# Requests for a weight tile one step sooner, and four casts moved ahead of two copies, in a fused linear-attention and low-rank-mixer kernel

## The chip, the cores and the metric

One core of a Trainium2 chip runs the whole kernel. The core has five engines that run side by side, each with its instructions in a fixed order: TensorE (PE in the profile; its weight loads are PEld), VectorE (DVE), ScalarE (ACT), GpSimd (POOL) and SyncE (SP). SP, and in places ACT, ask for transfers; sixteen DMA engines carry them out. The metric is the time of one execution on the device, in microseconds (us).

## The reference, cut to what matters

Two blocks follow each other. The first is linear attention with decay, 4 batches, 8 heads, 768 positions, head size 64, worked in blocks of 64 positions with a running state:

```python
intra = (qb @ kb.T * Dmask) @ vb                 # per head; Dmask = lam ** (i - j), i >= j
inter = (qb * lam_pow) @ kv_state
out[:, :, block] = intra + inter
kv_state = lam ** 64 * kv_state + (kb * rev_pow).T @ vb
```

Its output, heads side by side, is x with 4 x 768 rows of 512. The second block mixes positions by a low-rank product (rank 32) and then channels by a two-layer network (512 to 2048 to 512):

```python
u = x + (x.T @ U @ V).T
out = u + np.maximum(u @ w_ch1, 0) @ w_ch2
```

U, V and both weight matrices arrive in double precision, so the kernel has to turn their 64-bit words into single precision itself.

## The kernel before, in words

The kernel keeps near-single precision on TensorE by splitting each operand of the large products into a high part and a low part (and a difference of them), so each large product is three matmuls.

It has two halves. The front (up to about 120 us) walks through 24 steps, one for each 128 rows: step s belongs to batch s // 6 and is its row tile c = s % 6 (NT is 6, NS is 24). The back is two long runs of matmuls, u @ w_ch1 (lines 833 and 844) and relu(...) @ w_ch2 (lines 965 to 969).

The order of the front is written out by hand, as a list of pieces per step (lines 648 to 681), under a manual schedule: an engine's instructions stand in the order in which the pieces issue them. What a step does, in that order:

- **turn, split** (lines 592 on): transposes of a finished row tile of u and their split into high and low parts, for the first product.
- **prep(s + 1)** (line 371): TensorE transposes q and k of the next step (L361); ScalarE copies them from PSUM, q first, then k (L367, qt and kt); SP asks for a later q.
- **next_of_low**: the next of a list of pieces for the low-rank rows of the batch just finished. For batches 0 to 2 the list has two pieces (lines 525 to 543). The first, own, casts four groups of rows to their high parts on ScalarE (L528), with the low parts subtracted on POOL behind each (L529). The second, other, copies the rows to a second set of partitions by four small transfers on SP (L539).
- **scale** on POOL (L392 for q, L381 for k), **mixed** on VectorE (L574).
- **intra, state, inter**: the block's products on TensorE. intra (L455) multiplies the masked scores with v, state (L427) makes the running state, inter (L466) uses the state before. A copy on ScalarE (L472) takes the result from PSUM. next_v asks for a later v on ScalarE's queue.
- the second **next_of_low**, in the first step of a batch.
- **scores(s + 1)** on TensorE (L408), and **masked(s + 1)** on VectorE (L417): the scores of the next step times the decay mask. So L408, L417 and the next step's L455 follow each other across three engines.
- **low** (L482, the low-rank product of a finished batch), **mix** (L562, the mixing of positions for a row tile of the batch before; for its first tile it stands at the end of the second step).
- **aside(s)**: a slice of side work, given by a table (lines 738 to 747). It holds the conversion of U, V and of the first two tiles of w_ch1.
- **store** of u and **next_k** on SP.

The side work of a tile of w_ch1 has twelve pieces: four requests for its words, a quarter each (L146, 128 KB, on SP); an extraction of the exponents on VectorE (one, L166), with two operations on ScalarE behind (L173, L174); the mantissa (L155); and two, three, four, five, six, seven, which assemble and split the value. The table says for each piece the step whose aside holds it. NS there means the pieces left over for after the front. In steps after the sixth the aside stands between scores and masked, so a piece of it on VectorE runs ahead of the mask of the next step.

The words of consecutive tiles alternate between two buffers. Tile 0's words are requested in steps 8 to 11 and extracted in step 12; tile 1's table row is the one that changes.

Of the kernel before, what the change touches and what calls it, by code (L numbers as in the profile page):

```python
# [18 lines left out]
def kernel(  # L19
# [32 lines left out]
    NT = S // P  # L52
# [7 lines left out]
    NS = B * NT  # L60
# [142 lines left out]
    def split_steps(tile_of, src, in_parts=False, scale=None, apart=False):  # L203

        st = {}

        def dst():
            if "w" not in st:
                st["w"] = wconv.tile([P, C], FP32, tag="wf", name="wf")
            return st["w"]  # L210

        def five():
            st["o"] = o = tile_of()
            st["t"] = o[:, 0, :].bitcast(FP32)
            on_scalar(lambda: nc.scalar.mul(o[:, 0, :], st["w"], NEAR))  # L215

        def six():
            w, low = st["w"], st["o"][:, 1, :]
            st["low"] = low.bitcast(FP32) if scale is None else w
            nc.vector.tensor_tensor(  # L220
                out=low if scale is None else w, in0=w, in1=st["t"], op=ALU.subtract
            )
            if scale is not None:
                on_scalar(lambda: nc.scalar.mul(low, w, scale))

        def seven():
            nc.vector.scalar_tensor_tensor(
                st["o"][:, 2, :], st["t"], -E, st["low"], ALU.mult, ALU.add
            )

        return weight_steps(dst, src, C, in_parts=in_parts, apart=apart) + [five, six, seven]
# [3 lines left out]
    def w1_steps(ft, in_parts=False, apart=False):  # L235
        def tile_of():
            w1v[ft] = w1_pool.tile([P, 3, C], F32R, tag="w1", name="w1")
            return w1v[ft]

        cols = moe_w_ch1[:, ft * P : (ft + 1) * P].rearrange("(c p) f -> p c f", p=P)  # L240
        return split_steps(tile_of, cols, in_parts, apart=apart)
# [407 lines left out]
    for s in range(NS):  # L649
        b, c = divmod(s, NT)  # L650
        done = s - NT - 1
        more = s + 1 < NS
        turns = done > 0 and (done - 1) // TG < FG
        mixes = 0 <= done < NS - NT - 1
        rows = c == 0 and b > 0
        step = [("fade", s)] * (c > 0)
        step += [("mix", done)] * (mixes and c != 1) + [("turn", done - 1)] * turns
        step += [("split", done - 1)] * turns
        step += [("prep", s + 1)] * more
        step += [("mix", done + 1)] * (not more)  # L660
        step += [("next_of_low", b - 1)] * rows
        step += [("scale", s + 1)] * more
        step += [("mixed", done)] * (mixes and c != 1)
        step += [("late", s - 1)] * (1 < s < NT - 1 or s > NT)
        step += [("turned", done - 2)] * (done > 1 and c == 1)
        step += [("mixed", done + 1)] * (not more)
        both = [("intra", s), ("state", s)]
        step += (both if s > NT else both[::-1]) + [("next_v", s), ("inter", s)]
        step += [("next_of_low", b - 1)] * rows
        step += [("late", s)] * (s < 2 or s in (NT - 1, NT))  # L670
        step += [("turned", done - 1)] * (done > 0 and c > 0)
        step += [("mix", done), ("mixed", done)] * (mixes and c == 1)
        step += [("scores", s + 1)] * more
        step += [("low", b)] * (more and c == NT - 1)
        step += [("aside", s)] * (0 < s < NT - 2 or s > NT)
        step += [("masked", s + 1)] * more
        step += [("low_rows", b)] * (more and c == NT - 1)
        step += [("aside", s)] * (s in (0, NT - 2, NT - 1, NT))
        step += [("store", done)] * (done >= 0 and done // TG < FG)
        step += [("next_k", s)] * (s > 0)  # L680
        pieces += step
# [15 lines left out]
    def v_steps():  # L697

        st = {}

        def dst():
            if "v" not in st:
                st["v"] = wconv.tile([P, C], FP32, tag="wf", name="vf")[0 : 2 * R, 0:SH]
            return st["v"]

        def parts(gs):
            for half in range(2):
                rows, cols = slice(half * R, (half + 1) * R), slice(half * SH, (half + 1) * SH)
                for g in gs:
                    yield v_hl[g * R : (g + 1) * R, cols], rows  # L710

        def five():
            st["t"] = t = wconv.tile([P, C], FP32, tag="wt", name="vt")[0 : 2 * R, 0:SH]
            nc.vector.tensor_scalar(
                t.bitcast(U32), st["v"].bitcast(U32), HI, None, ALU.bitwise_and
            )
            on_scalar(high)

        def high():
            for out, rows in parts((0, 2)):  # L720
                nc.scalar.copy(out, st["t"][rows])

        def low(g, engine):
            for out, rows in parts((g,)):
                engine.tensor_tensor(
                    out=out, in0=st["v"][rows], in1=st["t"][rows], op=ALU.subtract
                )

        halves = [moe_V[:, half * SH : (half + 1) * SH] for half in range(2)]
        return weight_steps(dst, halves, SH, 2 * R, in_parts=True) + [  # L730
            five, lambda: low(1, nc.vector), lambda: low(3, nc.gpsimd),
        ]
# [6 lines left out]
    for steps, at in (  # L739
        (u_side, (-1, 1, 1, 2, 2)),  # L740
        (v_steps(), (0, 0, 3, 3, 4, 4, 4, 5, 5)),
        (w1_steps(0, True, True), (8, 9, 10, 11, 12, 14, 15, 16, 17, 17, 20, 21)),
        (w1_steps(1, True, True), (15, 16, 17, 18, 18, 22, 23, NS, NS, NS, NS, NS)),
    ):
        assert len(steps) == len(at)
        for step, n in zip(steps, at):
            side.setdefault(n, []).append(step)
# [140 lines left out]
    c0, b = NS - NT, B - 1  # L888
# [180 lines left out]
```

## Time and profile before

| | |
|---|---|
| median of the runs | 659.63 us (659.31 to 661.56) |
| profiled execution | 657.43 us |
| its span in the trace | 655.6 us |
| TensorE busy | 640.6 us (98%) |
| TensorE's weight loads busy | 539.5 us (82%) |
| VectorE, ScalarE, POOL busy | 435.8, 268.6, 116.4 us |
| moved by DMA | 131.69 MB, mean 201 GB/s |
| requests for words of w_ch1 in quarters | 8 of 128 KB, 5.1 us to landing (median) |
| row copies L539 | 12 of 32 KB, 2.1 us to landing (median) |

Times in the text are counted from the start of the span. A line of the timeline gives start, duration, engine, source line, operation, output and inputs, and how many instructions are merged; in square brackets stands how long the engine was idle before it and what ended that. "SPq" and "ACTq" are requests for transfers, "PEld" the weight loads that go ahead of matmuls. In a line of the totals of waits stand the waiting engine and line, what it waited for, the total, the number of waits and the longest. "issue" means that no event shown in the profile ended the wait.

### The profile page before, as it was taken

The page shows a single profiled execution, that of the slowest core. Times are in us where ns is not written, and L with a number is a line of the kernel's source. Part 1 is how long each engine was busy: PE and PEld are TensorE (multiplying, and loading weights), DVE is VectorE, ACT ScalarE, POOL GpSimd, SP SyncE. Part 2 cuts the span into 40 slices and gives each one's busy share as a digit, 9 for nine tenths or more (in the row PEclk, how much of TensorE's full clock was granted, in tenths as well). Part 3 has the DMA queues.
Part 4 walks back from the last instruction along what each step waited for, and adds up shares of the span by engine and source line. Part 5 has one row for each costly group of instructions (what it writes and reads, how often), then busy time and mean ns, then how long its engine had stood idle before and what let it go on. Part 6 is the DMA issues. An engine that isn't in the chain of part 4 may idle for free.

```text
span 655.6 us, 13402 instructions
## 1 busy us (share of the span) xinstructions
PE 640.6 (98%) x5242; PEld 539.5 (82%) x5242; DVE 435.8 (66%) x713; ACT 268.6 (41%) x497; POOL 116.4 (18%) x104
## 2 busy tenths in 40 slices
PE   8999979999999999999999999999999999999997
PEld 7889968778888888888888888888888888888886
DVE  6766857676997777777798244585575665855854
ACT  4666756434664444444455131332232322322320
POOL 4475966331000000000000000030030210300300
PEclk9999998999999999999999999999999999999999
DMA  9989995155787556555576999865363363453521
GB/s 227 241 197 259 236 239 130 50 201 170 262 287 253 211 210 211 209 212 210 211 253 255 332 323 379 292 216 173 98 215 108 116 211 97 147 176 94 180 81 64
DMA packets 132737, 131.69 MB, mean 201 GB/s; under 512 B 81538, under 2 KB 90754, under 8 KB 132674
## 3 DMA queue, kind: packets, MB, share of 16 engines
q1 hardware_dynamic: 107552, 124.41, 58.4%
q10 hardware_dynamic: 25122, 6.42, 4.4%
q8 instruction: 41, 0.67, 0.4%
q14 instruction: 22, 0.18, 0.1%
HBM read 80.09 MB, written 50.33 MB: 199 GB/s over the span
## 4 chain that ended last, share of the span: by engine, by line
PE 93%; DVE 2%; DMA 1%; ACT 1%; issue 1%; POOL 0%; SPq 0%; ACTq 0%; DVEq 0%
PE pz L833 26%; PE pz L965 13%; PE pz L967 13%; PE pd L969 13%; PE pd L844 13%; PE px L455 3%; PE pss L408 3%; PE px L466 2%; PE pqk L361 1%; PE pkv L427 1%; PE pm L562 1%; DMA qraw<-in_q_dram 1%; PE pp L482 1%; PE pm L625 1%; DMA vp<-vp 0%
## 5 line engine op out<-in xcount | busy, mean ns | idle before, releaser
L833 PE MATMUL pz<-u_hl,w 128*128 128x512 f32 x768 | 184.5, 390 | 0.0
L833 PEld LDWEIGHTS pz<-u_hl,w 128*128 128x128 f32 x768 | 143.7, 188 | 30.0 <-ACT r L840 0.3
L967 PE MATMUL pz<-w_hl,m 128*128 128x512 f32 x384 | 148.6, 389 | 0.0
L965 PE MATMUL pz<-w_hl,m 128*128 128x512 f32 x384 | 148.2, 389 | 0.0
L969 PE MATMUL pd<-w_d,m 128*128 128x512 f32 x384 | 147.4, 389 | 0.0
L948 ACT ACTIVATE m<-rm 128x512 fp32r<-128x512 f32 x96 | 60.6, 632 | 183.1 <-PE pd L969 122.9
L949 DVE SCALAR_TENSOR_TENSOR m<-rm,m 128x512 fp32r<-128x512 f32 x96 | 71.5, 747 | 96.0 <-ACT m L948 96.0
L994 POOL TENSOR_TENSOR o<-o,u 128x512 f32<-128x512 f32 x20 | 29.7, 1521 | 433.3 <-DVE o L990 433.3
L849 DVE SCALAR_TENSOR_TENSOR r<-pd,r 128x512 f32<-128x512 f32 x96 | 61.7, 685 | 60.4 <-ACT r L840 48.2
L844 PE MATMUL pd<-u_d,w 128*128 128x512 f32 x384 | 95.9, 390 | 0.0
L969 PEld LDWEIGHTS pd<-w_d,m 128*128 128x128 f32 x384 | 72.1, 188 | 15.4 <-DVE m L950 0.3
L967 PEld LDWEIGHTS pz<-w_hl,m 128*128 128x128 f32 x384 | 72.1, 188 | 15.1
L965 PEld LDWEIGHTS pz<-w_hl,m 128*128 128x128 f32 x384 | 72.1, 188 | 14.7
L844 PEld LDWEIGHTS pd<-u_d,w 128*128 128x128 f32 x384 | 71.9, 188 | 14.8
L840 ACT ACTIVATE r<-pz 128x512 f32<-128x512 f32 x96 | 51.7, 590 | 64.4 <-PE pz L833 64.4
L950 DVE SCALAR_TENSOR_TENSOR m<-m 128x512 fp32r<-128x512 f32 x96 | 74.7, 780 | 3.0
L417 DVE TENSOR_TENSOR sm<-pss,mask 128x512 f32<-128x512 f32 x48 | 30.9, 684 | 16.7 <-PE pss L408 16.7
L215 ACT ACTIVATE w<-wf 128x512 fp32r<-128x512 f32 x32 | 20.3, 634 | 38.6 <-DVE wf L197 30.7
L455 PE MATMUL px<-vraw,sm 128*64 128x64 f32 x768 | 28.7, 229 | 5.6 <-issue 5.5
L455 PEld LDWEIGHTS px<-vraw,sm 128*64 128x64 f32 x768 | 25.8, 141 | 7.3 <-issue 5.8
L173 ACT ACTIVATE sc<-sc,ends 128x512 f32<-128x512 uint32 x30 | 21.6, 720 | 22.8 <-DVE sc L166 22.8
L408 PE MATMUL pss<-qt,kt 64*128 64x128 f32 x384 | 28.8, 289 | 0.0
(89 smaller groups left out, 608.5 us busy)
## 6 DMA issues: line engine op xcount, KB each, us to landing
r_d<-r SPq DMA_DIRECT2D x96, 256.0 KB, 2.4
rm<-r_d SPq DMA_DIRECT2D x96, 256.0 KB, 2.7
words<-in_moe_w_ch_dram SPq DMA_DIRECT2D x30, 512.0 KB, 4.3
w_d<-w SPq DMA_DIRECT2D x16, 768.0 KB, 3.4
w_hl<-w_d SPq DMA_DIRECT2D x16, 512.0 KB, 5.8
u_d<-x_nat SPq DMA_DIRECT2D x24, 256.0 KB, 4.0
u<-u_d SPq DMA_DIRECT2D x24, 256.0 KB, 4.3
qraw<-in_q_dram SPq DMA_DIRECT2D x23, 256.0 KB, 4.8
```

What stands on the lines that cost most here:

```text
L408: nc.tensor.matmul(out=pss[:, x, a, :], lhsT=kt[half[x], a, :], rhs=qt[half[x], a, :], start=True, stop=True,)
L455: nc.tensor.matmul(out=px[half[t], x, a, :], lhsT=sm[:, x, a, half[t]], rhs=vr[:, 2 * a + x, :], start=(a == 0), stop=(alone and a == HP - 1),
L833: nc.tensor.matmul(out=like(acc[g][0], g), lhsT=w[:, n, ct, :], rhs=columns(uhl[g][:, n], g, ct), start=(ct == 0 and n == 0), stop=(ct == ...
L840: nc.scalar.mul(rs[g], acc[g][0], 4096.0 + 1.0)
L844: nc.tensor.matmul(out=like(acc[g][1], g), lhsT=w[:, 2, ct, :], rhs=columns(ud[g], g, ct), start=(ct == 0), stop=(ct == CT - 1),)
L849: nc.vector.scalar_tensor_tensor(rs[g], acc[g][1], 4096.0, rs[g], ALU.mult, ALU.add)
L948: nc.scalar.activation(out=m[:, 0], in_=r, func=AF.Relu, scale=NEAR)
L949: nc.vector.scalar_tensor_tensor(m[:, 1], r, 0.0, hi, ALU.max, ALU.subtract)
L950: nc.vector.scalar_tensor_tensor(m[:, 2], hi, E, low, ALU.mult, ALU.subtract)
L965: nc.tensor.matmul(out=pz, lhsT=m[:, 0, cols], rhs=hl[:, 0], start=first, stop=False)
L967: nc.tensor.matmul(out=pz, lhsT=m[:, 1, cols], rhs=hl[:, 1], start=False, stop=end)
L969: nc.tensor.matmul(out=pd, lhsT=m[:, 2, cols], rhs=dd, start=first, stop=end)
```

## The change

Two edits. In the table, the four requests for tile 1's words move from steps 15, 16, 17, 18 to 14, 15, 16, 17; the extraction stays in step 18. In the list of pieces, for step 6 (the first step of the second batch, s == NT) the first next_of_low stands ahead of prep instead of behind it, so that ScalarE's four casts L528 come before its copies L367 of q and k for step 7; steps 12 and 18 keep the order they had.

```diff
         step += [("split", done - 1)] * turns
+        step += [("next_of_low", b - 1)] * (s == NT)
         step += [("prep", s + 1)] * more
         step += [("mix", done + 1)] * (not more)
-        step += [("next_of_low", b - 1)] * rows
+        step += [("next_of_low", b - 1)] * (rows and s > NT)
         step += [("scale", s + 1)] * more
...
         (w1_steps(0, True, True), (8, 9, 10, 11, 12, 14, 15, 16, 17, 17, 20, 21)),
-        (w1_steps(1, True, True), (15, 16, 17, 18, 18, 22, 23, NS, NS, NS, NS, NS)),
+        (w1_steps(1, True, True), (14, 15, 16, 17, 18, 22, 23, NS, NS, NS, NS, NS)),
```

TensorE, VectorE and POOL have the same instructions in the same order in both kernels. On ScalarE only the six instructions named change places. On SP the first request moves ahead of the store of u in step 14, each of the others likewise one step up, and none is left behind the four row copies of step 18.

## The prediction

> **What bounds the kernel now.** I read the page first, then the totals of waits, the chain, the timeline round the two places that the change touches, and a table of stretches. Three times are in play: the profiled execution took 657.43 us, its trace spans 655.6 us, and the median of the runs is 659.63 us (659.31 to 661.56), 2.2 above the profiled one. I work in the trace's own times and carry the difference to the median.
>
> The page's busy times, and the shares of the chain that ended last:
>
> ```profile
> PE 640.6 (98%) x5242; PEld 539.5 (82%) x5242; DVE 435.8 (66%) x713; ACT 268.6 (41%) x497; POOL 116.4 (18%) x104
> PE 93%; DVE 2%; DMA 1%; ACT 1%; issue 1%; POOL 0%; SPq 0%; ACTq 0%; DVEq 0%
> ```
>
> TensorE is the bound from end to end, so an edit on other engines matters only where TensorE stands still or runs slowly. From 152 us to the end the chain is matmuls of the two products; there is nothing there for this change. The totals of waits say where TensorE stands still:
>
> ```profile
> PE px L455 <- issue: 5.5, 3, 4.8
> DVE sc L166 <- DMA words<-in_moe_w_ch_dram: 5.0, 1, 5.0
> ...
> PE pm L562 <- DMA vp<-vp: 1.2, 1, 1.2
> ```
>
> One wait of 4.8 us before the intra-block products (L455), one of 5.0 us of VectorE for words of a weight tile, and one of 1.2 us for the low-rank rows. The timeline (start, duration, what) shows that the first two are one event, in step 18 (first block of the last batch):
>
> ```profile
> 86.03 2.17 SPq L146 DMA_DIRECT2D words<-in_moe_w_ch_dram  x1
> ...
> 92.56 1.16 PE L408 MATMUL pss<-qt,kt 64*128 64x128 f32 x16
> 92.56 3.03 SPq L539 DMA_DIRECT2D vp<-vp  x4
> ...
> 95.64 0.58 SPq L146 DMA_DIRECT2D words<-in_moe_w_ch_dram  x1
> ...
> 98.10 0.43 DVE L166 TENSOR_SCALAR sc<-words 128x512 uint32<-128x512 uint32 x1 [5.01 <-DMA words<-in_moe_w_ch_dram]
> 98.44 1.28 DVE L417 TENSOR_TENSOR sm<-pss,mask 128x512 f32<-128x512 f32 x2
> ```
>
> The reader sees a queue inside a queue. The fourth request for words stands on SP behind four row copies (L539, 3.03 us), so it goes out at 95.64 and lands at 97.98. VectorE, in order, waits for it from 93.08 to 98.10, and the masking of step 19 (L417), whose scores are ready at 93.72, stands behind. L455 needs that mask.
>
> **Part one: the four requests a step sooner.** Nothing is added: four requests of 128 KB go out in steps 14 to 17 in place of 15 to 18, each ahead of its step's store of u and the next k and q. On VectorE, ScalarE and POOL this part moves nothing. In step 18 only the extraction (L166) is left, behind the request of step 17, which stood third before: asked at 86.03, landed at 92.12, 6.09 us later. L166 could start at 93.08 anyway, and takes 0.43; the mask waits for the scores until 93.72. The words may thus land as late as 93.72 - 0.43 = 93.29 at no cost: 1.17 us of room.
>
> What the step costs then need not be guessed, since step 12, the same step one batch earlier, does the same work with its words in hand (the only one of the two with a wait is 18). Its lines, and the stretches of step 18 and 19 (length, busy times, then the granted clock of TensorE, DMA share, GB/s):
>
> ```profile
> 65.59 0.42 DVE L166 TENSOR_SCALAR sc<-words 128x512 uint32<-128x512 uint32 x1
> ...
> 67.14 1.24 PE L455 MATMUL px<-vraw,sm 128*64 128x64 f32 x32
> ...
> 72.23 1.15 PE L455 MATMUL px<-vraw,sm 128*64 128x64 f32 x32
> ```
>
> ```profile
> 94.46:99.23 4.77, 0.01 (x2) 0.03 (x1) 1.13 (x3) 1.79 (x4) 3.24 (x3) 0.74 0.63 174
> 99.23:102.06 2.83, 2.83 (x52) 2.71 (x55) 1.09 (x2) 0.77 (x2) 0.00 (x0) 0.50 0.55 123
> 102.06:105.82 3.76, 3.76 (x82) 3.49 (x84) 2.65 (x7) 2.01 (x6) 3.54 (x3) 0.80 0.46 113
> ```
>
> With the words there, the mask starts at 93.74 and L455 of step 19 follows 0.79 later, as in step 12 (mask 66.35, L455 67.14): 94.53 in place of 99.23, 4.70 us sooner. From there to L455 of the next step took 72.23 - 67.14 = 5.09 in the batch before, but 105.75 - 99.23 = 6.52 now, because the clock was granted at 0.50 and 0.80 after the standstill: 1.43 more. So part one is worth 4.70 + 1.43 = 6.13 us; I take 6.1.
>
> Bounds. Below: SP pushes the loads of steps 14 to 17 back by at most the longest issue of such a request seen in steps 15 to 17, 2.25 us; the words then land at 94.4 and cost 1.1 of the gain: 5.0. If their flight is also as long as the longest of the front (a k load, 7.30 against 6.09), another 1.2 goes: 3.8. Above: 6.2, since TensorE already works back to back in step 13. I take 6.1 because the steps 8 to 11, each with one request as 14 to 17 will be, ran at 4.31 us a step without a wait for a transfer.
>
> At one place the size hangs on a rule. The rows show the slow clock after an idle stretch of 4.77 us, and none after the 1.2 us wait. The Trainium skill, "TensorE: Matmul & The Clock Gate", section "Part 1: The HAM clock gate", says that the clock falls to half after an idle window of about 3.4 us, that the window runs free of the kernel, and that the slow time therefore varies from run to run. By that rule an unprofiled run might pay less than 1.43, and the sum of both parts could be as low as 5.4; by the trace's rows it is 6.8, and I keep the rows.
>
> The rest of the saved time must survive to the end. Loads for steps 19 to 23 hang on buffers that the same steps free, so they come earlier too; the copies of the low-rank rows for step 19 land at 96.86, and TensorE would reach their use (L562) at 94.53 + 69.50 - 67.14 = 96.89. That is met with nothing to spare, and a wait here, were a copy to take the longest landing of its kind (3.3 us from 95.01), would cost 1.4.
>
> **Part two: the rows' high parts first, in step 6.** Four casts (L528), 0.30 us each and 0.32 apart, now come ahead of the copies of q and k (L367). Nothing else is reordered on ScalarE, and no queue is passed on SP or POOL; their waits end sooner. These lines show the place:
>
> ```profile
> 35.51 0.59 ACT L367 COPY kt<-pqk 128x512 f32<-128x512 f32 x1
> ...
> 36.12 0.62 ACT L528 CAST vp<-p_f 32x128 fp32r<-32x128 f32 x2
> ...
> 36.41 1.16 PE L408 MATMUL pss<-qt,kt 64*128 64x128 f32 x16
> ...
> 42.23 0.50 PE L562 MATMUL pm<-vp 64*128 64x256 f32 x3 [1.17 <-DMA vp<-vp]
> ```
>
> The casts can start at 34.70 (the rows leave PSUM at 34.66) in place of 36.12. Loss: q's copy moves to 35.98 and k's ends at 37.06, 0.96 late; the scores of step 7 (L408), now at 36.41, start at 37.10, 0.69 late, and TensorE's next steps with them. Gain: the four POOL subtractions behind the casts and the four copies on SP behind those start about 1.4 sooner, so the last copy lands at about 42.18 - 1.4 = 40.8. TensorE reaches the second matmul of the mix at 40.86 (the first starts at 40.67, and one takes about 0.19) + 0.69 = 41.55, finds its rows there, and goes on where it went on at 42.23: 0.68 us sooner. The POOL product of q (L392) moves forward with its queue and stays clear of its use. Bounds: +1.17 if the scores lose nothing after all; -0.69 if the last copy, whose record is missing, keeps its old landing (the chain's 42.18) and TensorE's later work finds no slack. I take 0.7, next to the worked row.
>
> **Sum.** 6.1 + 0.7 = 6.8 us. The profiled execution would take 657.43 - 6.8 = 650.6, and the median, 2.2 above it, 659.63 - 6.8 = 652.8 us.
>
> **The rivals.**
> *The gain comes in part.* The words land late or the row copies become the next wait. For it: 1.17 us of room, no room at L562, and a stretch from 72.23 to 90.60 with the DMA engines full (285 GB/s, against 265 in steps 8 to 11). Against: steps 12 and 13. With 3.8 from part one and nothing from part two, 659.63 - 3.8 = 655.8.
>
> *The change does nothing.* L455 waits for something else, such as v or the earlier output copy. v landed at 87.49 and the copy ended at 94.11, while the first half of the mask ended at 99.08, just before 99.23. That nearly excludes it; the time would stay at 659.6.
>
> *Slower, by the DMA queues.* The engines are full in steps 14 to 17, and a fifth transfer a step could hold back q, k and v. It decides when k of step 18, asked at 76.10 behind the new request, lands after TensorE wants it: landing 80.55, use 84.80, so 4.25 us of room. The extra 128 KB at 285 GB/s is 0.46 us. Only if each of the four steps lost 2.5 us would it reach 659.63 + 10 - 6.8 = 662.8. The Trainium skill, "DMA: Bandwidth & Descriptors", section "Issuing engines are not separate DMA queues", speaks on this side: transfers of all queues share the same 16 engines and interleave, so asking sooner makes no bandwidth. The trace agrees that the engines are full there, and shows that the loads have the room.
>
> **How the numbers follow.** 0.5% of this kernel, 3.3 us, is about what a measurement can tell from no change. Chances: forecast 0.79, gain in part 0.10, nothing 0.05, slower 0.06. The forecast's own range is 651 to 654.5: 6.8 give or take the bounds nearest to it, with the runs' spread of about 1. The range given reaches from 650.5 (part two at its upper bound, 1.17, and a median closer to the profiled time) to 656.5, which takes in the partial gain. Faster by over 0.5% (below 656.3): 0.79 and nearly all of the partial case, 0.88; same 0.06; slower 0.06.
>
> **What would show it.** In the new profile L166 of step 18 starts within half a microsecond of 92.4 (93.08 less part two), with no wait for words; the longest wait before L455 is under 1 us; the granted clock stays at 1.00 between 92 and 105; L455 of steps 19 and 20 are about 5.1 apart. For part two, scores of step 7 at about 37.1 and L562 with no wait for the rows. It would be wrong if words land after about 92.6 in the new times, if L562 of step 19 waits, or if TensorE waits for q, k or v between 72 and 92.

## The result, and the profile after

The changed kernel took 650.97 us in the median (650.55 to 651.89, four runs), the kernel before 660.6 beside it (659.31 to 662.2). The ratio is 0.9855, with a 95% interval of 0.9827 to 0.9883: 9.6 us less, between 7.7 and 11.4. The ratios, here and below, leave out runs in a slower state of the chip, of which there was one, the 661.33 us of fourth_first. The measured median lies 1.8 us below the predicted 652.8, inside the wide range (650.5 to 656.5) and at the lower edge of the forecast's own (651 to 654.5). The profiled execution took 651.21 us, with a span of 649.4; the one before had 655.6, so between the two traces there are 6.2 us. The rest of this text is about what lies between 6.2 and 9.6, and about which of the two edits gave what.

Busy times and the shares of the chain, from the page of the kernel after:

```profile
PE 638.7 (98%) x5242; PEld 537.8 (83%) x5242; DVE 435.7 (67%) x713; ACT 268.4 (41%) x497; POOL 116.3 (18%) x104
PE 93%; DMA 3%; DVE 1%; ACT 1%; issue 1%; ACTq 0%; DVEq 0%; SPq 0%
```

TensorE still bounds the kernel, with the same number of instructions; VectorE's share of the chain went from 2% to 1%, and that of transfers from 1% to 3%, most of it where the second product starts (386 to 402 us). Of the totals of waits, two lines answer to those shown of before:

```profile
PE px L455 <- issue: 1.9, 4, 0.7
...
PE pss L408 <- ACT kt L367: 0.6, 1, 0.6
```

The waits of L166 for words (5.0 us) and of L562 for the row copies (1.2) are gone, and the longest wait before L455 fell from 4.8 to 0.7. A new one of 0.6 stands before the scores: step 7 now waits for k's copy. The timeline of the kernel after round step 18:

```profile
85.60 2.13 SPq L146 DMA_DIRECT2D words<-in_moe_w_ch_dram  x1
...
90.02 1.15 PE L455 MATMUL px<-vraw,sm 128*64 128x64 f32 x32
...
91.97 1.16 PE L408 MATMUL pss<-qt,kt 64*128 64x128 f32 x16
91.98 2.95 SPq L539 DMA_DIRECT2D vp<-vp  x4
92.42 0.42 DVE L166 TENSOR_SCALAR sc<-words 128x512 uint32<-128x512 uint32 x1
...
93.18 1.29 DVE L417 TENSOR_TENSOR sm<-pss,mask 128x512 f32<-128x512 f32 x2 [0.34 <-PE pss L408]
93.97 1.24 PE L455 MATMUL px<-vraw,sm 128*64 128x64 f32 x32
...
98.81 1.15 PE L455 MATMUL px<-vraw,sm 128*64 128x64 f32 x32
```

The last request goes out at 85.60, its words land at 90.86, and L166 takes them at 92.42 without a wait. The mask now waits for the scores and not for VectorE, and L455 of step 19 follows the mask 0.79 later. L455 of step 18 to that of step 20 took 15.15 us before and 8.80 now. In the timeline of the kernel before, step 18 begins here; step 20 follows at 105.75:

```profile
90.60 1.18 PE L455 MATMUL px<-vraw,sm 128*64 128x64 f32 x32
```

In the stretches of the kernel after between the starts of L455 in steps 18, 19, 20 and 21 (length, busy times, then granted clock, DMA share, GB/s) the clock stays at full speed:

```profile
90.02:93.97 3.95, 3.68 (x92) 3.39 (x89) 2.83 (x6) 3.85 (x11) 2.15 (x5) 1.00 0.93 225
93.97:98.81 4.84, 4.83 (x128) 4.54 (x128) 3.67 (x9) 4.30 (x11) 4.84 (x5) 1.00 0.81 188
98.81:103.27 4.46, 4.38 (x129) 4.10 (x125) 4.32 (x7) 3.33 (x9) 4.46 (x4) 1.00 1.12 284
```

And the place of the second edit, in step 6, from the timeline of the kernel after:

```profile
34.74 1.25 ACT L528 CAST vp<-p_f 32x128 fp32r<-32x128 f32 x4
...
36.50 0.59 ACT L367 COPY kt<-pqk 128x512 f32<-128x512 f32 x1
37.15 1.16 PE L408 MATMUL pss<-qt,kt 64*128 64x128 f32 x16 [0.62 <-ACT kt L367]
...
41.41 0.51 PE L562 MATMUL pm<-vp 64*128 64x256 f32 x4
```

The casts come first, k's copy ends at 37.09, the scores start 0.74 later than before (36.41), and the mix runs through its four matmuls in one piece. L455 of step 8 starts at 43.87 and not, as in the kernel before, at 44.69: the lost 0.74 came back, and 0.82 more. The line of the kernel before, from its timeline:

```profile
44.69 1.15 PE L455 MATMUL px<-vraw,sm 128*64 128x64 f32 x32
```

### The profile page after: what moved, and what is told of

Same layout as the page of the kernel before. It is cut to its first block, busy times and chain, and to the rows that moved or that the text cites. A ratio compares the mean times of both kernels' runs of the same rounds, so it can differ in the third digit from the quotient of the medians.

```text
span 649.4 us, 13406 instructions
## 1 busy us (share of the span) xinstructions
PE 638.7 (98%) x5242; PEld 537.8 (83%) x5242; DVE 435.7 (67%) x713; ACT 268.4 (41%) x497; POOL 116.3 (18%) x104
## 4 chain that ended last, share of the span: by engine, by line
PE 93%; DMA 3%; DVE 1%; ACT 1%; issue 1%; ACTq 0%; DVEq 0%; SPq 0%
PE pz L834 26%; PE pd L845 13%; PE pz L968 13%; PE pz L966 13%; PE pd L970 12%; PE pss L408 4%; PE px L455 4%; DMA rm<-r_d 2%; PE px L466 2%; PE pqk L361 2%; PE pkv L427 2%; PE pm L562 1%; DMA kraw<-in_k_dram 1%; PE pp L482 1%; PE pm L625 1%
## 5 line engine op out<-in xcount | busy, mean ns | idle before, releaser
L215 ACT ACTIVATE w<-wf 128x512 fp32r<-128x512 f32 x32 | 20.3, 633 | 38.6 <-DVE wf L197 30.7
L455 PE MATMUL px<-vraw,sm 128*64 128x64 f32 x768 | 28.5, 225 | 2.3 <-issue 1.9
L408 PE MATMUL pss<-qt,kt 64*128 64x128 f32 x384 | 28.9, 290 | 0.6 <-ACT kt L367 0.6
L455 PEld LDWEIGHTS px<-vraw,sm 128*64 128x64 f32 x768 | 25.4, 137 | 4.1 <-issue 3.3
```

The costliest lines, as they stand in the source:

```text
L408: nc.tensor.matmul(out=pss[:, x, a, :], lhsT=kt[half[x], a, :], rhs=qt[half[x], a, :], start=True, stop=True,)
L455: nc.tensor.matmul(out=px[half[t], x, a, :], lhsT=sm[:, x, a, half[t]], rhs=vr[:, 2 * a + x, :], start=(a == 0), stop=(alone and a == HP - 1),
```

## The experiments

The front was cut at the first L455 of steps 6, 8, 14, 18 and 20, which every one of these kernels has, and each trace read by these stretches. The table is worked out from the start times of these matmuls; a profiled execution stands in each row, so a row tells where time lies, and the medians below tell how much there is. The profiled executions of the nine kernels with early words lie 1.8 us above the medians of their runs on average, those of the five others under 0.5, so columns are to be compared with care. "Early rows" means the casts ahead of q's and k's copies (or off ScalarE), "early words" all four requests for words ahead of step 18.

| kernel (us) | to step 6 | 6 to 8 | 8 to 14 | 14 to 18 | 18 to 20 | 20 to end |
|---|---|---|---|---|---|---|
| before | 35.4 | 9.31 | 27.5 | 18.37 | 15.15 | 549.9 |
| before_again | 34.7 | 11.37 | 27.2 | 18.36 | 15.05 | 550.0 |
| busy_wait | 35.7 | 9.57 | 27.3 | 18.36 | 16.68 | 549.7 |
| fourth_first | 35.5 | 9.73 | 27.2 | 19.71 | 12.98 | 550.0 |
| casts_only (early rows) | 38.3 | 7.97 | 28.1 | 23.06 | 14.54 | 550.4 |
| requests_only (early words) | 38.3 | 9.72 | 28.2 | 21.07 | 9.04 | 550.8 |
| after (both, as all below) | 35.4 | 8.45 | 27.8 | 18.36 | 8.80 | 550.6 |
| after_again | 35.4 | 8.45 | 27.8 | 21.70 | 8.79 | 550.0 |
| after_third | 37.2 | 7.97 | 27.6 | 23.05 | 9.18 | 550.7 |
| all_in_14 | 38.6 | 7.98 | 28.0 | 20.13 | 8.78 | 550.4 |
| requests_12_13 | 35.5 | 8.47 | 28.0 | 19.86 | 9.08 | 550.0 |
| casts_on_dve | 38.0 | 7.92 | 28.2 | 19.18 | 9.35 | 551.2 |
| dve_15_16_16_17 | 36.2 | 7.87 | 28.2 | 19.82 | 9.64 | 549.7 |
| casts_every | 36.0 | 7.97 | 28.9 | 20.09 | 9.99 | 550.6 |

**The two kernels again.** Three rows are the kernel before and the changed one without an edit.

> The kernel before once more, unchanged. The median gain of the change (9.6 us) is larger than the 6.2 us by which the two traces differ. Theory one, the standstill varies: in a second profile of before the wait of step 18 for the fourth words is again 4 to 6 us, and if the execution is 2 to 4 us longer than the first profile's, the wait or the slow clock behind it is longer by about that much. Theory two, the extra lies elsewhere: the wait is again about 5.0 us and the span differs by a stretch away from step 18, for instance the start of the second product. Against the kernel before, 0 us by both, within 2 us.

> The changed kernel once more, beside the others on one chip. By the prediction the sum of the two parts alone: 6.8 us in the trace. By the theory that before's standstill is longer in other executions, 8 to 10 us in the timed runs again, and the spread of its own runs smaller than that of the kernel before.

> The changed kernel once more, timed beside the others of this group, to see what two earlier groups left apart (9.6 and 6.1 us below before). By the traces so far the step itself gives 6.2 to 6.9, and what lies between is stalls of TensorE that come and go: 0.5 to 2.2 us in the middle of a group of matmuls, where a packet of the instruction queue starts over 3 us after its page was entered, and up to 0.9 at step 15. Expected: a median 6 to 9 us below before; in its trace no wait for words, clock 1.00 at 92 to 105, and every TensorE gap over 0.5 us that no release ends stands at a late instruction packet.

Measured: before_again 659.43 us in the median, ratio 1.0001 (0.9979 to 1.0022). after_again 653.45 beside 659.45, ratio 0.9907 (0.9873 to 0.994). after_third 652.38 beside 659.46, ratio 0.9916 (0.9887 to 0.9945). All 16 runs of the changed kernel lie between 650.55 and 657.55, all 74 of the kernel before, before_again among them, between 656.26 and 665.75; the means are 653.1 and 659.8, 6.7 apart. Worked out from the runs' own scatter (2.1 and 1.7 us), that is 6.7 give or take 1.2. By means the three groups give 9.6, 5.7 and 5.8: the first, with four runs each, lay at the favourable end, and the 8 to 10 us that one theory expected of after_again did not come back. Nor did its trace show the expected 6.8 less than before: its span is 652.1, 3.5 less, and that of after_third is 655.7, as long as that of the kernel before.

The rows of the table say where a kernel scatters by 6 us in a front that is the same each time: 18 to 20 repeats within 0.4 us in the three traces of the changed kernel and within 0.1 in the two of the kernel before, while "to step 6" and "14 to 18" take 34.7 or 38, and 18.4 or 23, in kernels of both sorts. Eight of the nine with early words take over 18.4 there, and two of the five others. What happens in these two stretches is told below, under the unexpected.

The standstill of step 18 was again there in before_again, 5.1 us long. This run also showed something that the profile of before had not. It waited 1.85 us for the row copies in step 6 and not 1.2, and the clock fell behind that wait. Stretches of before_again, the wait and what follows it:

```profile
40.38:42.23 1.85, 0.00 (x1) 0.00 (x0) 0.00 (x0) 1.41 (x5) 1.85 (x2) 1.00 0.92 205
42.23:44.10 1.87, 1.87 (x19) 1.87 (x20) 0.69 (x1) 0.00 (x0) 0.24 (x1) 0.54 0.96 216
```

Steps 6 to 8 took 11.37 in this run against 9.31 in the first: 0.7 by the longer wait, and most of the rest by a clock near 0.55.

**Each edit by itself.** requests_only:

```diff
-        (w1_steps(1, True, True), (15, 16, 17, 18, 18, 22, 23, NS, NS, NS, NS, NS)),
+        (w1_steps(1, True, True), (14, 15, 16, 17, 18, 22, 23, NS, NS, NS, NS, NS)),
```

> Only the four requests a step sooner; the casts stay where they were. By the prediction: 6.1 us in the trace (4.7 of standstill, 1.4 of slow clock), no wait of L166, L455 of step 19 starts about 94.5; in the timed runs 6 to 9 us. By the rival that the two parts only work together: under 3 us.

casts_only:

```diff
         step += [("split", done - 1)] * turns
+        step += [("next_of_low", b - 1)] * (s == NT)
         step += [("prep", s + 1)] * more
...
-        step += [("next_of_low", b - 1)] * rows
+        step += [("next_of_low", b - 1)] * (rows and s > NT)
```

> Only the four casts ahead of the copies in step 6; the requests stay in steps 15 to 18. By the prediction: 0.7 us in the trace (scores of step 7 about 0.7 later, no wait of L562 for the rows), and the wait of L166 stays near 5 us. By the rival that the late scores eat the gain: 0 us, or slower by up to 0.7.

Measured: requests_only 654.38 us, ratio 0.9906 (0.987 to 0.9941); casts_only 658.02, ratio 0.9983 (0.9956 to 1.0009), both beside 659.45. Of the two stretches at which the edits aim, each edit moves its own alone: requests_only has 9.04 in steps 18 to 20 and keeps 9.72 in steps 6 to 8 with 1.6 us of wait at L562; casts_only has 7.97 in steps 6 to 8 and keeps 14.54 in steps 18 to 20 with 5.0 us of wait at L166. So neither part needs the other, and part one gives most of the gain. By its median requests_only gained 5.1 us, less than the 6 to 9 expected, and neither trace is shorter than that of the kernel before (spans of 657.1 and 662.4 beside 655.6): both lost 2.9 us ahead of step 6, and 2.7 and 4.7 in steps 14 to 18, to stops that are told below. Part two alone is within what the runs can tell from nothing, though its stretch gains 1.3 us over before.

**Which step holds the requests.** all_in_14 and requests_12_13 are the changed kernel with other rows in the table:

```diff
-        (w1_steps(1, True, True), (14, 15, 16, 17, 18, 22, 23, NS, NS, NS, NS, NS)),
+        (w1_steps(1, True, True), (14, 14, 14, 14, 18, 22, 23, NS, NS, NS, NS, NS)),
```

```diff
-        (w1_steps(1, True, True), (14, 15, 16, 17, 18, 22, 23, NS, NS, NS, NS, NS)),
+        (w1_steps(1, True, True), (12, 12, 13, 13, 18, 22, 23, NS, NS, NS, NS, NS)),
```

> As the changed kernel, but all four requests (512 KB) in step 14, where the DMA engines are full. By the slower rival (the loads of q, k and v are held back): SP is busy with the four for 4 to 8 us, k of step 18 lands after its use and TensorE waits for a load, 1 to 4 us slower than the changed kernel. By the prediction's room of 4.25 us: no wait for a load, or one under 1 us. By the theory that executions differ by TensorE's own instruction fetch: fetch packets that start over 2.5 us after the page is crossed, and stalls in the middle of a group of matmuls, 1 to 3 us in all between 74 and 92.

> As the changed kernel, but two requests in step 12 and two in step 13, behind the row copies, where the traces show the DMA engines idle for some 3 us. If the full stretch of steps 14 to 17 costs anything: the same 6 to 9 us faster than before with a smaller spread, and no instruction packet of TensorE over 2.5 us late between 74 and 92. If k and q behind the four requests become late (k of step 16 had 2.4 us of room): a wait of TensorE for k near 76, up to 2 us, and a median 0 to 2 us above the changed kernel's.

Measured, beside 660.07: all_in_14 653.67 us, ratio 0.9892 (0.9848 to 0.9937), and requests_12_13 653.29, ratio 0.9893 (0.9861 to 0.9925). Steps 18 to 20 take 8.78 and 9.08, as in the changed kernel. It is enough that all four are asked before step 18; asking still sooner brings nothing. TensorE waited for no load of q, k or v in all_in_14 either, with four transfers of 128 KB on top in one step, and the stops in the middle of a group of matmuls that one theory expected between 74 and 92 us did not come. What both show over 18.36 in steps 14 to 18 (20.13 and 19.86) is nearly all TensorE waiting behind a late copy of x on ScalarE, 0.5 to 0.9 us at a time, in two places of each (1.7 and 1.4 us together).

**The queue on SP.** fourth_first is the kernel before with only the fourth request issued ahead of the row copies in step 18:

```diff
+        step += [("fourth", s)] * (s == 3 * NT)
         step += [("next_of_low", b - 1)] * rows
...
-    run.update(aside=aside, late=on_scalar_late)
+    run.update(aside=aside, late=on_scalar_late, fourth=lambda s: side[s].pop(0)())
```

> The kernel before with one edit: in step 18 the fourth request for words is issued ahead of the four row copies, all other requests stay in steps 15 to 17, the casts stay where they were. If the standstill comes from the request's place behind the row copies on SP, as the prediction read it, then the request goes out about 3 us sooner (in before's times 92.6 in place of 95.64), its words land about 2.3 later at 94.9 to 95.4, VectorE's wait shrinks from 5.0 to 2 to 2.6 us, TensorE's standstill from 4.8 to 1.8 to 2.4, and the clock behind it is slow for less than before: L455 of steps 19 and 20 lie 5 to 6 us apart; the row copies themselves go out 0.6 later. Gain against before 2.5 to 3.8 us in the trace, and a median 2 to 4 us lower. No late ScalarE request for v in steps 15 and 16, since nothing was moved into step 14. If the wait came from full transfer engines alone, and not from the queue, the words would land near 98 all the same, the wait would stay near 5, and the time would be before's.

Measured: 655.48 us, ratio 0.9913 (0.9883 to 0.9943), a wide scatter of 651.32 to 661.33. The timeline of fourth_first:

```profile
92.34 0.93 SPq L146 DMA_DIRECT2D words<-in_moe_w_ch_dram  x1
...
94.02 3.54 SPq L539 DMA_DIRECT2D vp<-vp  x4
97.70 0.51 DVE L166 TENSOR_SCALAR sc<-words 128x512 uint32<-128x512 uint32 x1 [3.16 <-DMA words<-in_moe_w_ch_dram]
...
98.91 0.30 PE L455 MATMUL px<-vraw,sm 128*64 128x64 f32 x3 [2.99 <-issue]
```

Taken from the scores of step 19 (94.01 here, 92.56 before), the request goes out 4.75 us sooner, but its words land only 1.9 sooner: 5.2 us after the request, at 97.52, where the late request of the kernel before needed 2.3. The standstill shrinks from 4.77 to 2.99 and does not go; VectorE's wait fell from 5.0 to 3.2, and not to 2 to 2.6.

Full transfer engines are not the reason: their share was 0.62 from the request to the landing, and 0.54 for the late request of the kernel before. A landing is recorded in sixteen parts. Fifteen of them had come by 95.76, near the expected 94.9 to 95.4; the sixteenth came at 97.52. The last packet of the words started at 96.48, 0.99 after the one before it, and just as a packet of 16 KB with instructions ended, which had begun at 95.53. That this packet held it up is read from these times and was not tested. So the reading of the queue holds for fifteen parts of the words, and the last one cost 1.8 us of the gain in this execution.

The other runs say that it is not always so. Three of them (651.32 to 655.48) show a mean granted clock of 0.999 to 1.000, like the changed kernel, where the 18 runs of the kernel before beside them show 0.991 to 0.997: there was little slow clock left in them. A request of step 18 ahead of the row copies can thus be early enough, but nothing makes sure of it. In the profiled execution the standstill of 3 us is still long enough for a slow clock:

```profile
98.90:101.20 2.30, 2.29 (x48) 2.30 (x48) 1.10 (x2) 0.79 (x2) 0.45 (x1) 0.59 0.95 231
101.20:105.00 3.80, 3.80 (x86) 3.44 (x82) 2.53 (x7) 1.90 (x6) 3.47 (x3) 0.80 0.63 151
```

**The slow clock.** busy_wait is the kernel before with 36 matmuls that write an unused part of the output bank ahead of L455 in step 19, so that TensorE is busy while it waits.

```diff
     def intra(s):
...
+        for i in range(36 if s == 3 * NT + 1 else 0):
+            nc.tensor.matmul(
+                out=both[:, 0, 2 * P : 3 * P], lhsT=ident, rhs=ident, start=True, stop=True
+            )
```

> The kernel before, with 36 matmuls of 128x128 into unused columns of the output bank put in front of the intra products of step 19: they fill some 4 us of TensorE's standstill and change nothing that it waits for. By the theory that 1.4 us of the gain is the slow clock behind the standstill: the wait of L166 stays near 5 us, L455 of step 19 still starts near 99.2, but the granted clock stays near 1.00 behind it and L455 of steps 19 and 20 are 5.1 apart and not 6.5; 1.4 us faster in the trace at step 20. By the rival that the steps behind are slow for another reason (late transfers, POOL): still 6.5 apart, 0 us.

Measured: 661.08 us beside 660.07, ratio 1.0011 (0.998 to 1.0042). VectorE's wait for words is what it was, 5.0 us, and the clock does not fall (stretches of busy_wait):

```profile
94.00:99.00 5.00, 5.00 (x64) 4.93 (x60) 0.65 (x2) 2.07 (x5) 3.94 (x4) 1.00 0.62 168
99.00:102.00 3.00, 3.00 (x29) 3.00 (x29) 1.57 (x3) 1.26 (x2) 0.00 (x0) 1.00 0.73 166
102.00:106.00 4.00, 4.00 (x104) 3.75 (x104) 1.20 (x5) 0.75 (x3) 1.35 (x2) 1.00 0.04 9
```

The added matmuls took 8.30 us, 0.23 each, and ran past the wait: the mask started at 98.69, so L455 could have come 0.79 later at 99.48, and came at 102.94, 3.46 late. From there to the next step's took 4.64 us, where before took 6.52: 1.88 back. That makes 1.6 us slower, and the runs, 1.0 slower, agree within their interval. The mean granted clock of the ten runs bears this out, 0.995 to 1.000 with a median of 0.999, beside 0.992 to 0.997 with a median of 0.995 for the kernel before. So the slow clock is the standstill's doing. By this trace it costs 1.9 us in this place, by the prediction 1.4, by the changed kernel 1.7 (6.52 against 4.84). The 6.52 is the longest of its kind, though: behind the standstill the step took 6.05 in before_again, 5.90 in casts_only and 6.12 in fourth_first, against 4.83 to 5.40 in the nine kernels with early words.

**Where the casts run.** casts_on_dve takes step 6's casts off ScalarE:

```diff
-                nc.scalar.copy(at, rows)
+                if b == 0:
+                    nc.vector.tensor_copy(out=at, in_=rows)
+                else:
+                    nc.scalar.copy(at, rows)
```

> As the changed kernel, but the four casts of step 6 run on VectorE, idle there, so that ScalarE copies q and k at once. By the prediction's account of part two (the gain of 1.4 us less the 0.69 by which the scores wait for k's copy): scores of step 7 back at 36.4, no wait for k's copy, and no wait for the rows; 0.6 to 0.7 us more than the changed kernel in the trace at L562 of step 7. By the rival that the rows come too late without the late scores to hide them: a wait of L562 for the rows of 0.3 to 0.8 us takes the gain away.

dve_15_16_16_17 has this, and the requests in steps 15, 16, 16 and 17:

> The changed kernel with two edits: the four casts of step 6 run on VectorE, so that q's and k's copies on ScalarE are not held up, and the four requests for words go out in steps 15, 16, 16 and 17, so that none is in step 14. If the late v request of steps 15 and 16 (the wait of ScalarE for the semaphore that an earlier q load still holds) comes from the request moved into step 14, then v of step 15 is asked in time again, the copy of x behind it is not late, and TensorE loses nothing at step 15; v of step 16 or 17 may be hit in its place, which costs up to 0.9. The words are there before VectorE comes to them, no wait over 0.3 for them. Gain over the changed kernel: 0.5 by the casts, 0 to 0.9 by the requests, so 6.5 to 8 us below before. If instead full transfer engines make v late wherever the requests are, the trace shows the same delay of 1.3 us or more on ScalarE in step 16 or 17 and a time equal to that of the changed kernel.

Measured: casts_on_dve 652.66 us beside 660.07, ratio 0.989 (0.9854 to 0.9925); dve_15_16_16_17 652.95 beside 659.46, ratio 0.9911 (0.9885 to 0.9938). From L455 of step 6 to that of step 7 took 3.03 in both, as in the kernel before (3.03), and 3.73 in the changed kernel: the scores are no longer late. Steps 6 to 8 took 7.92 and 7.87, against 8.45. But two more traces of the casts on ScalarE, casts_only and after_third, have 7.97, so the half microsecond is not always there to be had, and the times don't tell the kernels apart. (With the casts first on ScalarE this stretch took 8.45 to 8.47 in the three traces that reached step 6 by 35.5 us, and 7.97 or 7.98 in the four that reached it later, which would fit a ScalarE that is further ahead by then. That was not tested.) For the requests, both expectations had room for what came: with none in step 14, v of step 15 was in time (ScalarE's copy of x idle 1.07 before it, as in the kernel before), but v of step 16 was asked at 84.66 and not about 82.6, and the copy behind it was late. TensorE lost nothing over 0.3 us by it in this trace. So moving the requests to other steps moves the late request for v; whether it costs less there, one trace can't say. Neither of these, nor requests_12_13, beats the changed kernel by anything the runs can show.

**Casts first in every batch.** casts_every does in steps 12 and 18 what the change does in step 6:

```diff
-        step += [("next_of_low", b - 1)] * (s == NT)
+        step += [("next_of_low", b - 1)] * rows
...
-        step += [("next_of_low", b - 1)] * (rows and s > NT)
```

> The changed kernel with the casts ahead of the copies of q and k in all three turns (steps 6, 12 and 18) and not in step 6 alone. In steps 12 and 18 no wait for the rows was left to remove, so by the prediction's reckoning each turn loses what step 6 loses, scores 0.69 us late, with no gain behind: 1.4 us slower than the changed kernel in the trace, the rows of step 19 safe by 1.4 more. The rival, that the late scores cost nothing because TensorE's later work absorbs them, gives no difference; and if the rows of step 19 were late in the changed kernel in unprofiled runs, it would be up to 1 us faster.

Measured: 654.27 us, ratio 0.9934 (0.9908 to 0.9959) to before, and 1.9 above after_third beside it, whose interval it overlaps. In step 18 the timelines differ, first casts_every, then after_third:

```profile
93.00 1.24 ACT L528 CAST vp<-p_f 32x128 fp32r<-32x128 f32 x4
...
94.74 0.59 ACT L367 COPY kt<-pqk 128x512 f32<-128x512 f32 x1
95.43 0.69 PE L427 MATMUL pkv<-vraw,ks 128*64 128x64 f32 x16 [1.39 <-POOL vp L529]
```

```profile
96.51 0.59 ACT L367 COPY kt<-pqk 128x512 f32<-128x512 f32 x1
...
97.21 0.69 PE L427 MATMUL pkv<-vraw,ks 128*64 128x64 f32 x16 [0.19 <-issue]
```

What is late is the state's product L427, ahead of the scores. It starts 0.10 and 0.11 after k's copy ends (95.33 and 97.10). The profile names POOL's subtraction, which ended 0.05 before it in casts_every; but in after_third L427 started before that subtraction was even done, so that name cannot be right. The code bears out ScalarE: in steps 12 and 18 the state takes a PSUM bank under the tag of q's and k's transposes, which the copies have to empty first, while in step 6 it takes another. So L427 waits 1.39 us and not 0.19 in step 18, and 0.34 in step 12. The loss is there, but not where I expected it. Part two pays where the rows are late, and costs up to 1.2 us where they are not.

## Why the prediction was right, and where its steps were off

*The median.* 652.8 was predicted; 650.97 came out, and 653.45 and 652.38 in two more groups. The sum, 6.8, agrees with the 6.7 of all the runs together, give or take 1.2. That the agreement is so close is partly luck: part two was put too low, and steps 14 to 18 were put at no cost. The difference of 9.6 in the first group is no measure of the change; 5.7 and 5.8 came after it.

*Part one, 4.70 + 1.43.* Right, in place and size. L166 started at 92.42 (about 92.4 was said), L455 of step 19 came 3.95 after that of step 18 and not 8.63, which is 4.68; the next step took 4.84 and not 6.52, which is 1.68 where 1.43 was said. The earlier batch, step 12, was the right measure for the undisturbed step. One row beside it was misread: steps 8, 9 and 10 took 4.31 us each, but step 11, with the low-rank product in it, took 5.55; that none of the four waited for a transfer is right. Over the traces 18 to 20 went from 14.5 to 15.2 down to 8.8 to 9.6, leaving out casts_every with its own delay.

*The clock.* That a run would pay nothing for the slow clock, which gave the lower sum of 5.4, did not come about in a trace: the three of the full standstill and the one of 3.0 us in fourth_first all show the slow clock behind it, and busy_wait shows none where TensorE was kept busy. But its price varies, as said above, and 1.43 came from the longest case: the kernel before stayed at half clock for 6.83 us (96.73 to 103.56), where each of the nine other slow stretches in the fronts of these traces lasted 3.41 or 3.42. But to read the rows as "none after the 1.2 us wait" left the range between 1.2 and 4.8 open, and 1.85 us was enough in before_again. The Trainium skill, "TensorE: Matmul & The Clock Gate", section "Part 1: The HAM clock gate", has an idle window of about 3.4 us; here the clock was at half behind 1.85 and 2.10 us of idleness. That it varies, the traces agree: stops of 1.94 us (after_again) and 2.10 (after_third) left the clock at 1.00.

*Part two, 0.68.* Right in its mechanism, and too small. Scores of step 7 at 37.15 (37.10 was said), no wait at L562, L455 of step 8 0.82 sooner. The mis-sized term is what the rows cost before: I took the one wait of 1.17, but the other kernels without early rows waited 1.44 to 1.85 there, once with the slow clock behind. Steps 6 to 8 went from 9.31 to 9.73 (11.37 once) down to 7.87 to 8.47, so the part is worth 0.8 to 1.9, and 3 in an execution like before_again. From L455 of step 6 to that of step 7, the late scores cost 0.70 in two of the traces of the changed kernel and 0.2 in the third, about the 0.69 that was said. So the upper bound of 1.17 would have been nearer, but not for its reason: the scores do lose time.

*"The rest of the saved time must survive to the end", and "shows that the loads have the room".* This is the weak step, though the prediction came out right. TensorE never waited for a load of q, k or v in steps 14 to 18, and the fear of 2.5 us in each step was groundless. But the prediction put these steps at no cost, and looked for a cost at TensorE's own loads alone. In five of the nine traces with early words TensorE waits there for work that stands behind a late request for v: 0.2, 0.8, 1.0, 1.4 and 1.7 us in all, so 0.6 on average over the nine. In the five traces with the requests where they were, it never does.

How much of part one is given back by the runs is open. In the median steps 14 to 18 took 18.37 in those five traces and 20.09 in the nine, but that 1.7 is not clear of chance. Stops without a release are in it, 0.9 to 3.7 us in five of the nine and 1.1 and 2.3 us in two of the five. And the columns "to step 6" and "8 to 14", where part one changes nothing (but for requests_12_13), differ between the same traces by 0.8 each. The two stretches at which the change aims gain some 7.5 us, by the medians of the changed kernel's three traces and of those without the edit in question (15.05 to 8.80 and 9.72 to 8.45). The runs gain 6.7, and the 0.8 between them lies within the interval of 1.2.

The trace of after happened to show none of it (18.36). Its 6.2 come from 0.86 in steps 6 to 8 and 6.35 in steps 18 to 20, less 0.04 ahead of step 6, 0.23 in a stall at 63.10 and 0.69 after step 20, of which 0.45 is the start of the second product.

The Trainium skill, "DMA: Bandwidth & Descriptors", section "Issuing engines are not separate DMA queues", which the prediction set beside this rival, says that transfers of all queues share the same 16 engines. No run here shows that the sooner requests made other transfers land later; what the traces show is a wait for a shared semaphore, told below.

*L562 of step 19, "met with nothing to spare".* Held: the last row copy landed at 96.20, the mix began at 96.34.

*The rivals.* "Does nothing" and "slower" fell. "In part" may be true in small, by what steps 14 to 18 give back, but not by the causes that the prediction named for it: the words landed in time, and the row copies did not become the next wait.

## What to carry to other kernels

An in-order engine that waits for a transfer passes its wait to everything behind it, so look at what stands behind the waiting instruction before looking at the transfer; and an undisturbed copy of the same step elsewhere in the trace priced this wait better than the bounds did. A transfer is there when its last part is: fourth_first got 4.75 us of head start and 1.9 of landing, for one part in sixteen, so a request needs room behind it and not just a place ahead in its queue. Where runs of one kernel scatter by 1%, cut several traces at the same instructions: stretches that repeat show what an edit does, and stretches that do not show what it sets off.

## What the runs showed of the hardware that was not expected

**TensorE stands still where its next block of instructions comes late.** The page lists a queue "instruction" with 41 packets and 0.67 MB, which is 16 KB each and 64 bytes for each of TensorE's 2 x 5242 instructions, so by this estimate a packet holds some 128 matmuls with their weight loads. Eleven of the fourteen traces show stops of 0.4 to 2.2 us in the middle of a group of matmuls, with no release named, and they stand at the same places in the program, among them matmuls 344, 469, 595, 1481, 1733, 1859, 1986, 2113 and 2618: whole multiples of about 126.4 apart. From the timeline and the stretches of casts_only:

```profile
89.21 0.62 PE L466 MATMUL px<-kv,qs 64*64 64x64 f32 x25
...
91.93 0.49 PE L466 MATMUL px<-kv,qs 64*64 64x64 f32 x7 [2.10 <-issue]
92.35 2.08 PE L408 MATMUL pss<-qt,kt 64*128 64x128 f32 x16
```

```profile
89.83:91.93 2.10, 0.00 (x1) 0.00 (x1) 1.28 (x1) 0.00 (x0) 0.73 (x1) 1.00 1.16 265
91.93:94.40 2.47, 2.47 (x27) 2.13 (x30) 0.00 (x0) 0.58 (x1) 0.00 (x0) 0.50 0.69 203
```

TensorE stops after 25 of 32 matmuls, at number 2113, with the transfer engines full (share 1.16), and goes on at half clock: scores that take 1.16 took 2.08. The packet for this place started at 89.46 in casts_only, 4.03 us after the place before it was passed (after_again 4.70 and a stop of 1.94; after 3.04 at 63.10 and 0.51); in the kernel before the same packet started 1.28 after, and nothing stopped. In the long stops TensorE goes on 2.2 to 2.5 us after its packet's start. Over the first 20 such places of each trace but busy_wait, 260 in all, this holds throughout: where the packet started 2.95 us or more after the place before was passed, there was a stop of over 0.33 us (19 of 19); where it started less than 2.3 after, there was none (201 of 201). In between there was one at 12 of 40. A stop of 1.8 to 2.2 at matmul 469, near 24.5 us, in five traces, with a slow clock behind it in four, is what sets 37 to 38 apart from 35 in the column "to step 6". The Trainium skill, "Runtime: NRT & Kernel Launch", section "Instruction fetch mechanics", says that instructions come in blocks of 16 KB by a transfer queue of their own, and that the cost of crossing from one to the next is mostly hidden; these traces agree on the blocks, and show up to 2.2 us that is not hidden, with a slow clock behind it at times. Why a packet starts late in one execution and not in another is open. Full engines alone are not enough: in the kernel before their share was 1.09 to 1.15 from 74 to 90 us, in all_in_14 1.23 from 86 to 90, and TensorE did not stop in either. No run changed the time of a packet alone. casts_only, which has no request in step 14, had one of the worst in steps 14 to 18, so early words are not needed for it.

**A request waits for the landing of another, since they share a semaphore.** The requests for transfers take eight semaphores in turn. In after_again ScalarE, about to ask for v in step 15, waits until 79.30 for the semaphore of a q load asked on SP at 72.66, which lands at 79.24. From its timeline:

```profile
72.66 1.29 SPq L282 DMA_DIRECT2D qraw<-in_q_dram  x1
...
79.34 0.37 ACTq L282 DMA_DIRECT2D vraw<-in_v_dram  x1
...
79.81 0.59 ACT L472 COPY x_nat<-px 128x512 f32<-128x512 f32 x1 [2.63 <-PE pss L408]
...
83.63 1.13 PE L408 MATMUL pss<-qt,kt 64*128 64x128 f32 x15 [0.84 <-DVE kv L435]
```

v itself is not wanted yet; but the copy of x stands behind its request on ScalarE, comes 1.6 us late, and what follows on ScalarE and VectorE is late with it until TensorE loses 0.84 us. In the timeline of the kernel before, the same request and copy, with the copy idle for 1.07 and not 2.63:

```profile
78.22 0.37 ACTq L282 DMA_DIRECT2D vraw<-in_v_dram  x1
...
78.87 0.58 ACT L472 COPY x_nat<-px 128x512 f32<-128x512 f32 x1 [1.07 <-PE px L466]
```

One more request ahead in the order turns the sharing by one place, so that v comes after a q load of the step before, which needed 6.6 us to land here. The same happened to a v request in six more of the nine traces with early words: all_in_14 (until 76.57, k landed at 76.55), requests_12_13 (75.68, q at 75.66) and dve_15_16_16_17 (84.62, q at 84.60), after waits of 1.8 to 3.5 us, and requests_only, casts_on_dve and after_third. The first 1.4 of such a wait cost nothing, since in the kernel before the request goes out that long after its semaphore is free; there, and in the other four traces with the requests where they were, the wait was never over 1.1 in steps 14 to 18. TensorE shows it as 0.5 to 0.9 at a time in four of the nine traces, 0.2 in requests_only, and nothing in the others.
